# Fourier mixing and a gated feed-forward block: order of the weight preparation in the first chunk, and of two row transfers

## The chip, the cores and the metric

The kernel runs on one core of one Trainium2 chip. The metric is the device time of the whole kernel in microseconds (us); the kernel before takes 620.24 us in the median of 4 runs (620.0 to 620.54).

## The reference

```python
def _attn_ref(x):                       # x: (8, 3008, 256)
    X = np.fft.fft(x, axis=1)
    X = np.fft.fft(X, axis=2)
    return X.real.astype(np.float32)

def _moe_ref(x, w_gate, w_val, w_out):  # 24064 tokens, 256 -> 1536 -> 256
    g = x @ w_gate
    gelu = 0.5 * g * (1.0 + erf(g * np.float32(1.0 / np.sqrt(2.0))))
    val = x @ w_val
    return (gelu * val @ w_out).astype(np.float32)
```

The real part of a two-dimensional Fourier transform of each of 8 batches is the input of a feed-forward block with a GELU gate. The tokens of a batch come in mirrored pairs, so the kernel computes only half of them through the transform, as an even part E and an odd part O of 128 channels each.

## The kernel before, in words

**The feed-forward part.** Each batch has 1505 columns of token pairs, in three chunks of 512, 512 and 481. A chunk is worked through in twelve slots, one for each block of 128 columns of the inner dimension (1536). There are 8 x 3 x 12 = 288 slots, numbered from 0; slots 0 to 11 are the first chunk of batch 0. In slot i TensorE does, in this order:

- `G(i)` (`l1_gate`, line 674): gate columns of E, then of O, into a `ps_g` buffer (two of them); ScalarE's GELU (line 690) reads it;
- `g(i-1)` (`l1_gate2`): one more matmul with the weights "M" (minus two times the O weights) makes the mirrored tokens' gate of the slot before; ScalarE's second GELU (line 699) reads it and frees the buffer;
- `V(i)` (`l1_value`) and `v(i-1)` (`l1_value2`): the value columns, into `ps_v` (three buffers). In slots 0 to 7 of the first chunk (`three`), the value goes the same way as the gate, with a third weight set `w_minus`, and VectorE multiplies by the GELU (lines 713 and 730). From slot 8 on, the mirrored value is got without a third matmul: VectorE computes `ve` (line 718) from the row EB of channel 128 and `yw`, the value weights of that channel, then lines 734 and 736, and GpSimd multiplies (line 738);
- pieces of the output product of the chunk before (line 763, for the first chunk its own first pieces, from slot 9);
- `fill(i)`: whatever else a table gives to this slot.

**The fills of the first chunk** prepare the weights. `make_w(i, f0, n, parts, engine, m_engine)` multiplies the raw weights of gate (i=0) or value (i=1) with a 128-channel matrix, two matmuls of 512 columns for n=512 (line 451), into one of the two `ps_dft` buffers, and copies the result into `W_sb` with ScalarE (`engine="A"`, line 457) or VectorE ("V", line 459). `parts` are E (0) and O (1). For O it can also make M, with ScalarE (line 468) or VectorE (line 470) from the same `ps_dft` buffer, or with GpSimd ("P", line 466) from `W_sb`. `make_yw` computes `yw` from value's O weights (line 482, copy on line 484). `tp_y(0, 0)` makes EB of the first chunk (line 615, copy on line 618), `ch` and `tp_e`/`tp_o` are the last two steps of the transform (lines 535 and 591; copies on 541, 543 and 601).

**The rows.** For later batches `tp_row(b)` writes the row of channel 128 to a buffer in DRAM, and `tp_rows(b, c0, n)` reads it back with two transfers issued by SyncE on line 642: to all 128 partitions of EB, and to one partition of O. For batch 1 it is called once per chunk, after that chunk's `tp_o`; for later batches once for all chunks. The first slot of a batch is 36 b. SyncE also issues the output stores (line 668), four or more to a store, and takes its instructions in the order of the program.

**The order is written by hand** (`plan` fills two tables, `feed` walks them); every engine takes its own instructions in program order. Within a slot, the stores of finished output pieces come before the fill, since `feed` runs `two` before `fill`.

Of the kernel before, what the change touches and what calls it, by code (L numbers as in the profile page):

```python
# [28 lines left out]
def kernel(  # L29
# [22 lines left out]
    HALF = (NK - 1) * K1 + K1H  # L52
# [4 lines left out]
    def width(k2):  # L57
        return K1H if k2 == 0 else K1

    chunk_len = [sum(width(k2) for k2 in gr) for gr in groups]  # L60
    chunk_off = [sum(chunk_len[:i]) for i in range(NG)]
# [83 lines left out]
    def psum(tag):  # L145
        bufs = {"g": 2, "v": 3, "o": 1, "dft": 2}[tag]
        return psum_pool.tile([128, 512], FP32, tag=tag, bufs=bufs, name=f"ps_{tag}")
# [330 lines left out]
    def make_yw():  # L478
        def run():
            ps = psum("dft")  # L480
            for i in range(NFC):
                nc.tensor.matmul(
                    ps[:, i : i + 1], W["v", "O"][0:1, i * 128 : (i + 1) * 128], one_h, start=True, stop=True)
            nc.scalar.activation(yw[:, :], ps[:, 0:NFC], AF.Copy)
        return run
# [38 lines left out]
    def ch(b, pp, engine="A", qs=(0, 1)):  # L524

        def run():
            st = state(b)
            A = st["A"]
            if "Z" not in st:
                st["Z"] = Z_tile()  # L530
            ps = ps_any(b)
            for i, q in enumerate(qs):
                k = 2 * (2 * pp + q)
                for g in range(2):
                    nc.tensor.matmul(  # L535
                        ps[:, i * C : (i + 1) * C], _sub(A, [[1, 128]], g * NK * K1 + k * K1), II[:, g, :, :],
                        start=g == 0, stop=g == 1)
            n = len(qs) * C
            dst = _sub(st["Z"], [[1, n]], pp * 512 + qs[0] * C)
            if engine == "A":  # L540
                nc.scalar.activation(dst, ps[:, :n], AF.Copy)
            else:
                nc.vector.tensor_copy(dst, ps[:, :n])
        return run
# [39 lines left out]
    def tp_e(b, gi, g=0, engine="A", tag=None):  # L584
        def run():
            st = state(b)
            if b not in EO_bufs:
                EO_bufs[b] = EO_tiles()
            ps = psum(tag) if tag else ps_any(b)
            for pair, o, n in pairs(gi):  # L590
                nc.tensor.matmul(  # L591
                    ps[:, o : o + n], st["Z"][:, pair, g * 128 : g * 128 + 128], _sub(TP, [[1, n]], g * 128),
                    start=True, stop=True)
            if b == 0 and g == 1:
                for pair, o, n in pairs(gi):
                    nc.tensor.matmul(
                        ps[0:1, o : o + n], st["Z"][:, pair, 128:129], _sub(TP, [[1, n]], 0), start=True, stop=True)
            n = chunk_len[gi]
            dst = _sub(EO_bufs[b][g], [[1, n]], chunk_off[gi])
            if engine == "A":  # L600
                nc.scalar.activation(dst, ps[:, :n], AF.Copy)  # L601
            else:
                nc.vector.tensor_copy(dst, ps[:, :n])
        return run

    def tp_y(b, gi):

        def run():
            st = state(b)
            if b not in EB_bufs:  # L610
                EB_bufs[b] = EB_tile()
            n = chunk_len[gi]
            ps = ps_any(b)
            for pair, o, w in pairs(gi):
                nc.tensor.matmul(
                    ps[:, o : o + w], _sub(st["Z"], [[0, 128]], pair * C + 128), _sub(TP, [[1, w]], 0),
                    start=True, stop=True)
            nc.scalar.activation(_sub(EB_bufs[b], [[1, n]], chunk_off[gi]), ps[:, :n], AF.Copy)
        return run
# [18 lines left out]
    def tp_rows(b, c0, n):  # L638
        def run():
            y = yrow_dram[b % 2]  # L640
            for dst, rows in ((EB_bufs[b], 128), (EO_bufs[b][1], 1)):
                nc.sync.dma_start(
                    out=_sub(dst, [[1, n]], c0, part_num=rows),
                    in_=ap_replace(y, ap=[[0, rows], [1, n]], offset=y.offset + c0))
        return run

    def tp_o(b, gi, engine="A"):
        return tp_e(b, gi, 1, engine)
# [240 lines left out]
    def plan():  # L889

        fill, pool = {}, {}

        def at(table, s, f):
            table.setdefault(s, []).append(f)

        early = []
        for gi in (1, 2):
            e = "A" if gi == 1 else "V"
            early += [ch(0, 2 * gi), ch(0, 2 * gi + 1, e), tp_e(0, gi), tp_o(0, gi, e), tp_y(0, gi)]
        for s, f in (  # L900
                (0, make_w(0, 256, 256, m_engine="P")), (0, make_w(1, 256, 256, engine="V", m_engine="P")),
                (1, make_w(1, 512, 512, (1,), m_engine="P")), (1, lambda: load_wo(0)), (1, lambda: load_wo(1)),
                (2, make_w(0, 512, 512, (0,), "V")), (3, make_w(0, 512, 512, (1,))), (3, make_w(1, 512, 512, (0,), "V")),
                (4, make_w(1, 1024, 512, (1,), "V")), (5, make_w(0, 1024, 512, (0,), "V")),
                (5, make_yw()), (6, make_w(0, 1024, 512, (1,))), (6, tp_y(0, 0)), (7, make_w(1, 1024, 512, (0,), "V"))):
            at(fill, s, f)
        for i, f in enumerate(early):
            at(fill, (7, 8, 9, 10, 11, 12, 13, 14, 15, 16)[i], f)


        at(fill, 7, lambda: nc.sync.dma_start(
            out=ap_replace(yrow_dram[0], ap=[[0, 1], [1, 64]]), in_=EB_bufs[0][0:1, 0:64]))
        for k, s in ((0, 8), (1, 9), (2, 9)):
            at(fill, s, lambda k=k: load_part(2, k, (load_forward,)))
        for k, s in ((0, 18), (1, 19), (2, 19)):
            at(fill, s, lambda k=k: load_part(2, k, (load_mirror,)))

        taken = set()

        def spread(b, s0, s1):  # L920

            items = [tp_row(b)] + [f(b, gi) for gi in range(NG) for f in (tp_e, tp_o)]
            for i, f in enumerate(items):
                s = s0 + (i * (s1 - s0) // (len(items) - 1) if b > 1 else (0, 2, 3, 6, 8, 11, 13)[i])
                at(fill, s, f)
                taken.add(s)
                if b == 1 and i and i % 2 == 0:
                    at(fill, s + 1, tp_rows(b, chunk_off[i // 2 - 1], chunk_len[i // 2 - 1]))
            if b > 1:
                at(fill, s + 1, tp_rows(b, 0, HALF))  # L930

        for b in range(1, B):
            s0 = (b - 1) * NS
            ops = []
            for j0, nj in PIECES:
                ops += fold_ops(b, j0, nj, nc.gpsimd)
            per = len(ops) // 5
            first, n = (s0 - 19, 30) if b == 3 else (s0 - 22, 32)
            slot_of = [first + i * n // len(ops) for i in range(len(ops))]
            if b == 2:  # L940
                slot_of = [26, 27, 29, 30, 31, 33, 34, 37, 38, 39, 41, 42, 43, 45, 46, 49, 50, 50, 51, 51]
            if b == 1:
                slot_of = [4, 4, 5, 5, 6, 6, 7, 7, 8, 8, 9, 13, 13, 14, 15, 15, 16, 17, 17, 18]
            for s, f in zip(slot_of, ops):
                at(pool, s, f)
            if 1 < b < B - 1:
                for k, piece in ((0, 1), (1, 3), (2, 4)):
                    at(fill, slot_of[piece * per + 1] + 1, lambda b=b, k=k: load_part(b + 1, k))
            s = s0 - 9 if b > 1 else 12
            for i, (jg, piece) in enumerate(((2, 1), (1, 2), (0, 3), (3, 4))):  # L950
                ready = slot_of[piece * per + per - 1] + 2
                for g in range(2):
                    s = max(s + 1, ready)
                    while s in taken:
                        s += 1
                    at(fill, s, s1t(b, jg, g))
                if i == 2:
                    at(fill, s + 1, z_write(b, 0, 12))
                if i == 3:
                    at(fill, s + 1, z_write(b, 12, 4))  # L960
            at(fill, s + 2, z_read(b))
            if b == 1:
                spread(b, s + 7, s + 20)
                continue
            assert s + 7 < s0 + NS - 10
            spread(b, s + 7, s0 + NS - 5 if b == 2 else s0 + NS - 6)
        return fill, pool
# [71 lines left out]
```

## Time and profile before

| | |
|---|---|
| median of 4 runs | 620.24 us |
| the profiled execution, its own time | 620.08 us |
| its span | 618.2 us |
| TensorE matmuls busy | 609.7 us, 99% |
| VectorE busy | 576.5 us, 93% |
| GpSimd busy | 508.7 us, 82% |
| ScalarE busy | 425.0 us, 69% |
| granted TensorE clock | 1.0 |
| data moved | 65.40 MB, mean 106 GB/s |

The busy time of TensorE counts a matmul from its start to a modelled end, and matmuls overlap, so that small delays between two of them hide inside "busy". What tells them is the distance from one start to the next. A line of the timeline gives the start, the duration, the engine, the kernel's line, the operation with output and inputs, the count, and in brackets the idle time before it with what ended it. "PE" is the matmul, "PEld" the weight load, "DVE" VectorE, "ACT" ScalarE, "POOL" GpSimd, "SPq" SyncE's queue.

### The profile page before, as it was taken

To read this page: it belongs to the slowest core of one execution; us is meant where nothing else is said; L and a number is where in the kernel's file an instruction comes from. 1 tells how busy PE (TensorE), PEld (TensorE's weight loads), DVE (VectorE), ACT (ScalarE), POOL (GpSimd) and SP (SyncE) were. 2 spreads that over 40 slices of the span, in tenths; PEclk is the share of its full clock that TensorE was granted. 3 is DMA by queue.
4 is the path that set the end of the run, shared out by engine and by line. 5 is a ranking of instruction groups with operands and counts; after the bars stand their busy time and mean duration, and the time that the engine had idled before them with its cause. 6 is when DMAs were issued, how large, how long until landed. Compare 5 with 4: busy or idle time off the path is not lost.

```text
span 618.2 us, 12794 instructions
## 1 busy us (share of the span) xinstructions
PE 609.7 (99%) x4230; PEld 405.8 (66%) x4230; DVE 576.5 (93%) x940; ACT 425.0 (69%) x825; POOL 508.7 (82%) x513
## 2 busy tenths in 40 slices
PE   8999999999999999999999999999999999999997
PEld 4456666666666666666666666666666666666666
DVE  8789998999999999999999999999999999999992
ACT  7787667677766677676767677666776667666651
POOL 8989899999997999879997899969987555555561
PEclk9999999999999999999999999999999999999999
DMA  9952825546372354532553344533123312211123
GB/s 178 201 130 57 232 60 148 145 110 186 84 174 73 91 153 116 150 95 58 156 149 94 110 97 116 143 104 97 42 69 79 100 50 52 64 49 43 40 52 82
DMA packets 52466, 65.40 MB, mean 106 GB/s; under 512 B 7629, under 2 KB 47278, under 8 KB 50004
## 3 DMA queue, kind: packets, MB, share of 16 engines
q1 hardware_dynamic: 45472, 49.03, 30.4%
q0 software_dynamic: 6608, 15.29, 11.4%
q8 instruction: 33, 0.54, 0.4%
q10 hardware_dynamic: 320, 0.26, 0.2%
q14 instruction: 33, 0.27, 0.1%
HBM read 39.65 MB, written 30.17 MB: 113 GB/s over the span
## 4 chain that ended last, share of the span: by engine, by line
PE 93%; ACT 2%; DVE 2%; DMA 1%; issue 1%; SPq 0%; POOLq 0%; POOL 0%; ACTq 0%; DVEq 0%
PE ps_o L763 39%; PE ps_g L674 29%; PE ps_v L674 20%; PE ps_dft L555 2%; PE ps_dft L591 2%; DMA out_dram<-out_sb 1%; PE ps_dft L451 0%; DMA O_sb<-yrow 0%; ACT A_sb L519 0%; SPq L668 0%; DVE h_sb L730 0%; PE ps_dft L535 0%; DVE W_sb L459 0%; ACT G L351 0%; ACT L426 0%
## 5 line engine op out<-in xcount | busy, mean ns | idle before, releaser
L738 POOL TENSOR_TENSOR h_sb<-gelu_sb,v_sb 128x512 bf16<-128x512 bf16 (+1 forms) x280 | 319.8, 1147 | 90.8 <-DVE v_sb L736 78.6
L763 PE MATMUL ps_o<-Wo_sb,h_sb 128*128 128x256 bf16 (+1 forms) x2232 | 334.5, 273 | 0.0
L763 PEld LDWEIGHTS <-h_sb 128*128 128x128 bf16 (+1 forms) x2304 | 228.7, 100 | 111.2 <-POOL h_sb L738 1.2
L690 ACT ACTIVATE gelu_sb<-ps_g 128x512 bf16<-128x512 f32 (+1 forms) x288 | 169.5, 589 | 99.7 <-PE ps_g L674 93.5
L718 DVE SCALAR_TENSOR_TENSOR ve_sb<-EB_sb,yw,ps_v 128x512 f32<-128x512 bf16 (+1 forms) x280 | 206.1, 736 | 20.9 <-PE ps_v L674 17.1
L674 PEld LDWEIGHTS <-W_sb 128*128 128x128 bf16 x1440 | 138.0, 98 | 81.8 <-issue 4.1
L734 DVE TENSOR_TENSOR h_sb<-gelu_sb,ps_v 128x512 bf16<-128x512 bf16 (+1 forms) x280 | 189.7, 677 | 1.4 <-ACT gelu_sb L699 1.0
L736 DVE SCALAR_TENSOR_TENSOR v_sb<-ve_sb,ps_v 128x512 f32<-128x512 f32 (+1 forms) x280 | 187.2, 669 | 0.0
L674 PE MATMUL ps_g<-O_sb,W_sb 128*128 128x512 bf16 (+1 forms) x576 | 168.9, 374 | 0.6 <-DMA O_sb<-yrow 0.4
L699 ACT ACTIVATE gelu_sb<-ps_g 128x512 bf16<-128x512 f32 (+1 forms) x288 | 168.8, 586 | 0.0
L674 PE MATMUL ps_v<-E_sb,W_sb 128*128 128x512 bf16 (+1 forms) x288 | 108.0, 375 | 0.7 <-DVE W_sb L459 0.6
L674 PE MATMUL ps_g<-E_sb,W_sb 128*128 128x512 bf16 (+1 forms) x288 | 108.0, 375 | 0.7 <-ACT gelu_sb L699 0.3
L674 PE MATMUL ps_v<-O_sb,W_sb 128*128 128x512 bf16 (+1 forms) x288 | 108.0, 375 | 0.0
L783 ACT ACTIVATE out_sb<-ps_o 128x512 f32<-128x512 f32 x92 | 55.0, 598 | 34.4 <-PE ps_o L763 34.1
L229 POOL TENSOR_TENSOR eo_sb<-ab_sb 94x512 bf16<-94x512 f32 (+1 forms) x70 | 77.6, 1111 | 0.4
L558 ACT ACTIVATE S_sb<-ps_dft 96x512 bf16<-96x512 f32 x56 | 33.0, 589 | 18.6 <-PE ps_dft L555 18.6
L222 POOL TENSOR_TENSOR ab_sb<-x_raw,x_raw 94x508 f32<-94x508 f32 (+1 forms) x30 | 33.0, 1100 | 0.0
L225 POOL TENSOR_TENSOR ab_sb<-x_raw,x_raw 94x508 f32<-94x508 f32 (+1 forms) x30 | 33.0, 1099 | 0.0
L555 PE MATMUL ps_dft<-eo_sb,G 94*96 94x256 bf16 x119 | 22.3, 272 | 0.0
L601 ACT ACTIVATE E_sb<-ps_dft 128x512 bf16<-128x512 f32 (+1 forms) x23 | 13.5, 588 | 8.9 <-PE ps_dft L591 8.9
L163 POOL DMA_INDIRECT x_raw<-in_x_dram,idx x18 | 17.2, 956 | 2.9 <-issue 0.8
L601 ACT ACTIVATE O_sb<-ps_dft 128x512 bf16<-128x512 f32 (+1 forms) x22 | 13.0, 589 | 7.5 <-PE ps_dft L591 7.0
(151 smaller groups left out, 205.2 us busy)
## 6 DMA issues: line engine op xcount, KB each, us to landing
out_dram<-out_sb SPq DMA_DIRECT2D x364, 64.0 KB
x_raw<-in_x_dram SPq DMA_DIRECT2D x10, 768.0 KB
Z_sb<-z SPq DMA_DIRECT2D x7, 768.0 KB
z<-S_sb SPq DMA_DIRECT2D x7, 576.0 KB
EB_sb<-yrow SPq DMA_DIRECT2D x6, 376.2 KB
z<-S_sb SPq DMA_DIRECT2D x7, 192.0 KB
x_raw<-in_x_dram SPq DMA_DIRECT2D x2, 640.0 KB
x_stage<-in_x_dram SPq DMA_DIRECT2D x1, 768.0 KB
```

The source lines that it names most:

```text
L222: eng.tensor_tensor(ab(0, 1, up), fwd(1, up), mir(255, down), op=ALU.add)
L229: eng.tensor_tensor(_sub(eo, [[C, nj], [1, 128]], j0 * C + g * 128), ab(0, 0, [[1, 128]]), ab(1, 0, [[1, 128]]), op=op)
L555: nc.tensor.matmul(ps[:96, q * C : (q + 1) * C], G[:, j, :], _sub(eo, [[1, C]], j * C), start=(j == js[0]), stop=(j == js[-1]))
L674: nc.tensor.matmul(ps[:, :n], W[nm, part][:, fs], src, start=start, stop=stop, **kw)
L690: nc.scalar.activation(gl[:, 0, :n], pg[:, :n], AF.Gelu)
L699: nc.scalar.activation(_sub(gl, [[-1, n]], TOK + n - 1), pg[:, :n], AF.Gelu)
L718: nc.vector.scalar_tensor_tensor(ve[:, :n], EB_bufs[b][:, c0 : c0 + n], yw[:, fc : fc + 1], pv[:, :n], op0=ALU.mult, op1=ALU.add)
L734: nc.vector.tensor_tensor(st["h"][:, fc, 0, :n], gl[:, 0, :n], pv[:, :n], op=ALU.mult)
L736: nc.vector.scalar_tensor_tensor(_sub(vv, [[-1, n]], n - 1), ve[:, :n], 2.0, pv[:, :n], op0=ALU.mult, op1=ALU.subtract)
L738: nc.gpsimd.tensor_tensor(st["h"][:, fc, 1, :n], gl[:, 1, :n], vv[:, :n], op=ALU.mult)
L763: nc.tensor.matmul(pso[:m, half], st["h"][:, fc, sign, h0 : h0 + m], Wo_sb[:, fc, :], start=(fc == 0 and not (first and sign)), stop=(fc = ...
L783: nc.scalar.activation(_sub(osb, [[1, 2 * C]], 0, part_num=m), pso[:m, :], AF.Copy)
```

## The change

Three things. In the first chunk's fills, value's E columns 512 to 1023 move from slot 3 to slot 2 and those from 1024 on from slot 7 to slot 5; two M sets move from ScalarE to VectorE, and `ch(0, 2)` is copied by VectorE in place of ScalarE. `make_yw` and `tp_y(0, 0)` move one slot later. And `tp_rows` of all batches is put in the slot of the transform step before it, one slot sooner.

```diff
-            early += [ch(0, 2 * gi), ch(0, 2 * gi + 1, e), tp_e(0, gi), tp_o(0, gi, e), tp_y(0, gi)]
+            early += [ch(0, 2 * gi, "V" if gi == 1 else "A"), ch(0, 2 * gi + 1, e), tp_e(0, gi), tp_o(0, gi, e), tp_y(0, gi)]
         for s, f in (
                 (0, make_w(0, 256, 256, m_engine="P")), (0, make_w(1, 256, 256, engine="V", m_engine="P")),
                 (1, make_w(1, 512, 512, (1,), m_engine="P")), (1, lambda: load_wo(0)), (1, lambda: load_wo(1)),
-                (2, make_w(0, 512, 512, (0,), "V")), (3, make_w(0, 512, 512, (1,))), (3, make_w(1, 512, 512, (0,), "V")),
-                (4, make_w(1, 1024, 512, (1,), "V")), (5, make_w(0, 1024, 512, (0,), "V")),
-                (5, make_yw()), (6, make_w(0, 1024, 512, (1,))), (6, tp_y(0, 0)), (7, make_w(1, 1024, 512, (0,), "V"))):
+                (2, make_w(1, 512, 512, (0,))), (2, make_w(0, 512, 512, (0,), "V")),
+                (3, make_w(0, 512, 512, (1,), m_engine="V")),
+                (4, make_w(1, 1024, 512, (1,), "V")),
+                (5, make_w(1, 1024, 512, (0,))), (5, make_w(0, 1024, 512, (0,), "V")),
+                (6, make_yw()), (6, make_w(0, 1024, 512, (1,), m_engine="V")), (7, tp_y(0, 0))):
             at(fill, s, f)
...
                 if b == 1 and i and i % 2 == 0:
-                    at(fill, s + 1, tp_rows(b, chunk_off[i // 2 - 1], chunk_len[i // 2 - 1]))
+                    at(fill, s, tp_rows(b, chunk_off[i // 2 - 1], chunk_len[i // 2 - 1]))
             if b > 1:
-                at(fill, s + 1, tp_rows(b, 0, HALF))
+                at(fill, s, tp_rows(b, 0, HALF))
```

## The prediction

> **What bounds the kernel now.** I read the page first, then the waits, then the timeline where TensorE waits.
>
> ```profile
> span 618.2 us, 12794 instructions
> PE 609.7 (99%) x4230; PEld 405.8 (66%) x4230; DVE 576.5 (93%) x940; ACT 425.0 (69%) x825; POOL 508.7 (82%) x513
> PE 93%; ACT 2%; DVE 2%; DMA 1%; issue 1%; SPq 0%; POOLq 0%; POOL 0%; ACTq 0%; DVEq 0%
> ```
>
> TensorE is the bound, and 93% of the chain that ended last is its own. The change neither adds nor removes a matmul, so it can only gain where TensorE waits. The distances between matmul starts say how much that is: unhindered, 512 columns take 0.216 us, 256 take 0.109, 128 take 0.056. What exceeds these sums to some 15 us, of which 7.3 lie ahead of 20 us (the opening, untouched) and 3.5 after 100 us. The waits name the rest:
>
> ```profile
> PEld L674 <- DVE W_sb L459: 1.7, 2, 1.1
> PE ps_v L674 <- DVE W_sb L459: 0.6, 1, 0.6
> PEld L674 <- ACT W_sb L457: 0.5, 1, 0.5
> PE ps_g L674 <- DMA O_sb<-yrow: 0.4, 1, 0.4
> PE ps_g L674 <- ACT gelu_sb L699: 0.3, 1, 0.3
> ```
>
> In the timeline these are four places. Slot 4 (starts at 25.00), twice:
>
> ```profile
> 24.77 0.60 ACT L457 ACTIVATE W_sb<-ps_dft 128x512 bf16<-128x512 f32 x1 [0.21 <-PE ps_dft L451]
> 25.00 0.38 PE L674 MATMUL ps_g<-E_sb,W_sb 128*128 128x512 bf16 x1
> 25.41 0.68 DVE L459 CAST W_sb<-ps_dft 128x512 bf16<-128x512 f32 x1
> 25.42 0.60 PE L674 MATMUL ps_g<-O_sb,W_sb 128*128 128x512 bf16 x2
> 26.14 0.39 PE L674 MATMUL ps_v<-E_sb,W_sb 128*128 128x512 bf16 x1
> ```
>
> The O matmul could start at 25.22 and waits for gate's O columns, 0.205 us; V(4) could start at 25.86 and waits for value's E columns, 0.278. Then the start of slot 8, behind ScalarE, and V(8):
>
> ```profile
> 33.39 0.62 ACT L699 ACTIVATE gelu_sb<-ps_g 128x512 bf16<-128x512 f32 x1
> 34.06 0.38 PE L674 MATMUL ps_g<-E_sb,W_sb 128*128 128x512 bf16 x1 [0.34 <-ACT gelu_sb L699]
> 34.76 0.68 DVE L459 CAST W_sb<-ps_dft 128x512 bf16<-128x512 f32 x1
> 35.50 0.39 PE L674 MATMUL ps_v<-E_sb,W_sb 128*128 128x512 bf16 x1 [0.63 <-DVE W_sb L459]
> ```
>
> From start to start they lose 0.502 and 0.792 us. Last, slot 36, batch 1's first:
>
> ```profile
> 88.99 0.58 SPq L642 DMA_DIRECT2D EB_sb<-yrow  x1
> 89.62 0.29 SPq L642 DMA_DIRECT2D O_sb<-yrow  x1
> 91.66 0.38 PE L674 MATMUL ps_g<-E_sb,W_sb 128*128 128x512 bf16 x1
> 92.47 0.58 PE L674 MATMUL ps_g<-O_sb,W_sb 128*128 128x512 bf16 x2 [0.43 <-DMA O_sb<-yrow]
> ```
>
> O could start at 91.88 and starts at 92.47: 0.595 us. Slot 38 starts 0.152 late as well (96.50), behind ScalarE.
>
> **What the Trainium skill says.** "TensorE: Matmul & The Clock Gate", section "Wait — 56ns, not 53.3ns?", gives N/2.4 GHz plus 2.5 ns from start to start, 215.7 ns for 512 columns: the trace has 0.216. "PSUM — Partial Sum Buffer", section "PSUM bank collisions raise a hardware error", says that two engines must not access one bank at once, reads by ScalarE and VectorE included; so M on VectorE has to follow ScalarE's copy out of the same ps_dft buffer, and in the order of the changed kernel line 470 does wait for ScalarE. No pair like this stands in the first chunk before. "DMA: Bandwidth & Descriptors", section "Anatomy of one DMA — SWDGE (gpsimd) path", puts about 2 us of fixed cost on a transfer, mostly its completion; here the one-partition O row, behind SyncE's queue, takes 2.81 us from issue to landing.
>
> **The first chunk, slot by slot.** I walk the in-order queues with the trace's durations: ScalarE and VectorE start 0.42 us after the start of the last 512-column matmul that they need; a ScalarE instruction lasts 0.60 and lets the next start after 0.49; VectorE 0.68 and 0.60; a matmul that waits starts 0.05 after the end of what it waits for. With these the order before gives slot 4, 8, 9, 10 at 25.01, 34.00, 36.26, 38.09; the trace has 25.00, 34.06, 36.38, 38.20. One floor follows: in each slot the first GELU starts 0.22 + 0.42 = 0.64 us after the slot's start, the second 0.49 later, at 1.13, and ends at 1.73; the next slot's gate needs the buffer that it frees, and so opens 1.78 us after this one at the soonest, though six matmuls and one make_w are only 8 x 0.216 = 1.73.
>
> With the new order:
> - Slots 2 and 3. Slot 2 has two make_w (ten matmuls, 2.16), slot 3 one (1.78 by the floor): slot 3 opens at 23.22, slot 4 at 25.00 as before. The same matmuls, moved.
> - Slot 4. Value's E columns are there. But gate's O columns, first of slot 3's two fills before, are now at the end of slot 3: matmuls at 24.51 and 24.73, copy from 25.15 to 25.75, O matmul at 25.80 in place of 25.22. It loses 0.59, where before the slot lost 0.48. So this slot gains nothing, it loses 0.1. Slot 5: 27.36.
> - Slot 5 has two make_w; ScalarE copies one, VectorE the other: 2.16. Slot 6: 29.52.
> - Slot 6: six matmuls 1.29, yw 0.48 (from 28.96 to 29.44 before), make_w 0.43. Slot 7: 31.73. ScalarE copies yw (0.18) and gate's O to 32.57; VectorE's M follows, 32.62 to 33.30.
> - Slot 7: six matmuls, tp_y 0.22, then ch, whose ps_dft buffer M frees at 33.30: a wait of 0.07. ScalarE has only EB to copy (before: a weight copy and M, 31.37 to 32.55, then EB and the copy for ch). Slot 8 opens at 33.75 without the 0.50.
> - Slot 8: V(8) has its columns since slot 5, the 0.79 goes. Its 1.51 us of matmuls are below the floor, so slot 9 opens at 33.75 + 1.78 = 35.52 (a wait of 0.26). Slot 10: 37.30.
>
> 38.09 - 37.30 = 0.79 us of gain, 0.8. Bounds: 0.4, if the O wait in slot 4 and the floor each take 0.2 more; 1.1, if ScalarE is 0.3 sooner in slot 4. The price of M on VectorE (line 470, PSUM to bf16) isn't in the trace at 512 columns; the 256-column one at 17.64 took 0.47, a 512 cast 0.68. I take 0.68; at 0.95 (twice 0.47) ch in slot 7 waits 0.27 longer; at 0.47 its 0.07 go.
>
> **Cover.** The three VectorE instructions per slot (1.8 us) fit the slots of 1.78 to 2.16 with room from the slots before. Behind M of slot 6 stand lines 713 (slot 7), 730 (slot 6) and the copy for ch. 730 ends near 34.5 and V(9) needs its ps_v buffer at 36.2; the Z copy ends near 35.1 and tp_e reads it at about 37: 1.7 and 1.9 us of cover. EB is there at 34.1; line 718 wants it at 34.85. GpSimd runs without a gap to 39.47, whatever TensorE does, so its first product (line 738, slot 8) stays at 39.5, although its input comes 0.8 sooner; it was idle 1.07 and 0.59 before the next two, so by slot 10 it follows TensorE again. Its later combine (52.35 to 54.84) is read by TensorE at 55.36: 0.5 us of slack, kept if GpSimd moves along, as it is anchored by its product at 45.37, before which it idled 0.69. The small yrow transfer (line 911) behind EB goes from 33.06 to some 34.1, and the x_raw loads queued behind it on SyncE too; the folds of batch 2 that read them start in slot 26: no cost.
>
> **The rows.** In slot 33, not 34, two DMAs (0.58 and 0.29 us of issue) pass the four stores of 86.56 to 88.95. SyncE is free from 82.83. EB then waits only for the row's write, issued at 78.19; O waits for the ScalarE copy at 84.04 to 84.64. Even with their times from before (EB 88.99 to about 93.6, 4.6 us; O 2.81) they land by 88, and TensorE wants O at 91.88: the 0.595 goes whole. The stores come about 0.9 us later, four to an output buffer; three buffers rotate with some 6 us each, and no copy of line 783 waits for a store before. The later calls go one slot sooner and end no wait of TensorE; for batch 2 they pass stores as well, and O can hold SyncE for one copy of 0.6 us, at no cost for the same reason. The 0.152 at 96.50 may be a sequel or not: between 0 and 0.15; I take 0.
>
> Sum: 0.8 + 0.6 = 1.4 us. 620.08 - 1.40 = 618.7 for a profiled execution; the median stands 0.16 higher, so 618.8.
>
> **Rivals.**
> 1. The first chunk's gain is eaten by ScalarE, whose copy of gate's O columns in slot 4 now ends last; or GpSimd doesn't follow and TensorE waits at 55.36 for 0.8 - 0.5 = 0.3 us or more. For: the new 0.59 wait and the 0.5 us of slack. Against: slots 7 and 8 lose 1.3 us of waits for visible causes. Gain 0.6 to 1.1: 619.4.
> 2. More than summed: the wait of 96.50 goes too and slot 4 waits only as before. Gain 1.4 + 0.15 + 0.2: 618.5.
> 3. The rows bring nothing, since EB or O wait for something else in slot 33. Against: the order shows only the write, a queue entry and the copy. Gain 0.8: 619.4.
> 4. Slower: in slot 6 VectorE's M, held by ScalarE's copy, holds lines 713, 730 and the Z copy. TensorE waits from 1.7 us of delay on, one for one; to end 0.2% slower M would have to be late by 1.7 + 1.4 + 1.2 = 4.3 us, that is 621.5. ScalarE has no such backlog in that slot.
>
> **Numbers.** 0.2%, 1.24 us, is about what a measurement of this kernel can tell from no change: 619.0. Case as summed 0.55, rival 1 0.16, rival 2 0.15, rival 3 0.10, rival 4 0.04. The first falls below 619.0 with nine tenths, rival 2 wholly: 0.65 faster; 0.31 within; 0.04 slower. The range takes in rival 2 and most of 1 and 3: 618.2 to 619.7.
>
> **What would show it.** Right: no wait on W_sb by line 459, no wait on yrow; V(8) straight after slot 8's gate; the O matmul of slot 4 waiting 0.6 for line 457; slot 10 near 37.3; slot 37 (94.40 before) near 93.0. Wrong: a slot 4 that opens late, a new wait of line 555 on eo_sb, of line 763 on h_sb, or of line 783 on stores.

## The result, and the profile after

The changed kernel takes 619.38 us in the median of 41 runs (618.57 to 621.2), the kernel before 620.69 in 62 runs (619.45 to 622.75). The ratio is 0.9981, with a 95% interval of 0.9975 to 0.9986: faster by 1.2 us, between 0.9 and 1.6. The forecast was 1.4 us, from 620.2 to 618.8. So direction and size came out, but the runs show that the two parts of the sum did not share it as the prediction says.

The page of the changed kernel, its first lines and the granted clock:

```profile
span 617.3 us, 12798 instructions
PE 608.8 (99%) x4230; PEld 406.9 (66%) x4230; DVE 578.1 (94%) x941; ACT 424.9 (69%) x824; POOL 508.4 (82%) x513
PEclk8999999999999999999999999999999999999999
```

TensorE is the bound as before. The span is only 0.9 us shorter than the 618.2 of before; the 8 at the head of the clock line marks a slower opening, in which part of the gain is hidden, and the last section comes back to it. The waits of the changed kernel that have to do with weights:

```profile
PEld L674 <- ACT W_sb L457: 1.0, 1, 1.0
PE ps_g L674 <- ACT W_sb L457: 0.4, 1, 0.4
DVE W_sb L470 <- ACT W_sb L457: 0.4, 1, 0.4
```

The waits on VectorE's copies of line 459 (1.7 and 0.6) are gone from this view, and so is every wait on yrow. One wait on ScalarE's copy has grown instead. The timeline of the changed kernel shows it in slot 4:

```profile
25.50 0.38 PE L674 MATMUL ps_g<-E_sb,W_sb 128*128 128x512 bf16 x1
25.66 0.60 ACT L457 ACTIVATE W_sb<-ps_dft 128x512 bf16<-128x512 f32 x1 [0.21 <-PE ps_dft L451]
26.29 0.75 DVE L470 TENSOR_SCALAR W_sb<-ps_dft,keep 128x512 bf16<-128x512 f32 x1
26.31 0.60 PE L674 MATMUL ps_g<-O_sb,W_sb 128*128 128x512 bf16 x2 [0.43 <-ACT W_sb L457]
26.75 0.38 PE L674 MATMUL ps_v<-E_sb,W_sb 128*128 128x512 bf16 x1
```

Slot 4 opens at 25.50; its O matmul, wanted 0.216 later, starts 0.81 later, when gate's O columns have been copied. V(4) then follows at once, for value's E columns are there. (With their moves their copies also go from VectorE to ScalarE: the new lines have no "V".) The M set on VectorE (line 470) starts as ScalarE's copy ends. Slots 8 and 9 of the changed kernel:

```profile
34.31 0.38 PE L674 MATMUL ps_g<-E_sb,W_sb 128*128 128x512 bf16 x1
34.96 0.38 PE L674 MATMUL ps_v<-E_sb,W_sb 128*128 128x512 bf16 x1
35.44 0.59 ACT L699 ACTIVATE gelu_sb<-ps_g 128x512 bf16<-128x512 f32 x1
36.08 0.38 PE L674 MATMUL ps_g<-E_sb,W_sb 128*128 128x512 bf16 x1
```

V(8) starts 0.65 us after the slot, where it took 1.44 before; slot 9 opens 1.77 later, right after the second GELU: the floor. And the rows, on SyncE's queue of the changed kernel:

```profile
80.05 2.42 SPq L668 DMA_DIRECT2D out_dram<-out_sb  x4
82.56 0.53 SPq L642 DMA_DIRECT2D EB_sb<-yrow  x1
84.31 0.26 SPq L642 DMA_DIRECT2D O_sb<-yrow  x1
86.19 2.40 SPq L668 DMA_DIRECT2D out_dram<-out_sb  x4
88.97 0.35 SPq L157 DMA_DIRECT2D x_raw<-in_x_dram  x1
```

They now lie between two stores. The O row's completion is recorded at 85.68, 5.8 us ahead of its use in slot 36.

Since the opening differs from one execution to the next, the traces are best compared from the start of slot 1 on. The table gives all of them: the start of slot 1 in us, then how much later slots 8, 10, 38 and the last one (287) open, and the margin of the O row in the first slots of batches 1 and 2, which are slots 36 and 72 (from its landing to its unhindered use, 0.216 us after the slot's start; below zero TensorE waits). Its numbers are read from the starts of the first gate matmul of each slot and from the completion records of the transfers. The ratio is that of the timed runs to those of the kernel before, with its 95% interval; the second trace of before has no timed runs with it. Of these intervals, only those of "rows only" and "load later" lie clear of the interval in the first row of the changed kernel. So what a part is worth is read from the slot starts, and each kernel but two has one trace.

| kernel | slot 1 | +8 | +10 | +38 | +287 | margin batch 1, 2 | ratio |
|---|---|---|---|---|---|---|---|
| before | 19.29 | 14.77 | 18.91 | 77.21 | 581.39 | -0.55, 0.29 | 1 |
| before, again | 20.84 | 14.77 | 18.91 | 76.62 | 581.42 | 0.06, -0.48 | |
| changed | 19.81 | 14.50 | 18.04 | 75.59 | 579.88 | 5.8, 6.0 | 0.9981 (0.9975 to 0.9986) |
| changed, again | 19.29 | 14.50 | 18.04 | 75.59 | 579.85 | 5.6, 6.0 | 0.9984 (0.9976 to 0.9991) |
| rows only | 20.14 | 14.77 | 18.91 | 76.62 | 580.72 | 5.7, 6.1 | 0.9996 (0.9988 to 1.0005) |
| first chunk only | 19.50 | 14.50 | 18.04 | 75.62 | 579.99 | 0.01, 0.23 | 0.9993 (0.9985 to 1.0001) |
| load later | 20.27 | 14.77 | 18.91 | 76.62 | 581.09 | 0.29, 0.23 | 0.9999 (0.9989 to 1.0008) |
| M on ScalarE | 20.25 | 14.84 | 18.36 | 76.87 | 581.06 | 5.6, 6.1 | 0.9988 (0.9980 to 0.9995) |
| ch on ScalarE | 19.79 | 14.50 | 18.09 | 75.80 | 579.92 | 5.6, 6.2 | 0.9989 (0.9980 to 0.9998) |
| yw, tp_y as before | 20.05 | 15.06 | 18.59 | 76.41 | 580.67 | 5.6, 6.1 | 0.9992 (0.9979 to 1.0005) |
| value's E in slot 7 | 20.19 | 14.84 | 18.38 | 75.93 | 579.95 | 5.7, 6.0 | 0.9977 (0.9968 to 0.9987) |
| gate's O first | 20.78 | 13.92 | 17.46 | 75.12 | 579.41 | 5.6, 6.2 | 0.9974 (0.9965 to 0.9983) |
| ... and pieces sooner | 19.29 | 13.91 | 17.69 | 74.85 | 579.12 | 5.6, 6.1 | 0.9966 (0.9955 to 0.9977) |
| ... and Z later | 20.89 | 13.93 | 17.71 | 75.10 | 579.39 | 0.23, 6.2 | 0.9975 (0.9967 to 0.9983) |

### The profile page after: what moved, and what is told of

It is laid out like the page before. It is cut to its first block, busy times and chain, and to the rows that moved or that the text cites. A ratio compares the mean times of both kernels' runs of the same rounds, so it can differ in the third digit from the quotient of the medians.

```text
span 617.3 us, 12798 instructions
## 1 busy us (share of the span) xinstructions
PE 608.8 (99%) x4230; PEld 406.9 (66%) x4230; DVE 578.1 (94%) x941; ACT 424.9 (69%) x824; POOL 508.4 (82%) x513
## 4 chain that ended last, share of the span: by engine, by line
PE 95%; DMA 2%; ACT 1%; DVE 1%; issue 0%; POOL 0%; POOLq 0%; SPq 0%; ACTq 0%; DVEq 0%
PE ps_o L763 39%; PE ps_g L674 30%; PE ps_v L674 20%; PE ps_dft L555 2%; PE ps_dft L591 2%; DMA xb<-in_x_dram,idx 1%; DMA out_dram<-out_sb 1%; PE ps_dft L451 1%; PE ps_o L832 0%; PE ps_dft L535 0%; POOLq L1036 0%; ACT gelu_sb L699 0%; POOL h_sb L738 0%; PE ps_v L513 0%; ACT gelu_sb L690 0%
```

## Experiments

**One part alone.** Theory: the first chunk brings 0.8 us and the rows 0.6. The rivals are that one of them brings nothing.

Rows only:

```diff
-                    at(fill, s + 1, tp_rows(b, chunk_off[i // 2 - 1], chunk_len[i // 2 - 1]))
+                    at(fill, s, tp_rows(b, chunk_off[i // 2 - 1], chunk_len[i // 2 - 1]))
...
-                at(fill, s + 1, tp_rows(b, 0, HALF))
+                at(fill, s, tp_rows(b, 0, HALF))
```

> The kernel before with only the row transfers moved (all batches). Theory: the wait of slot 36 for the O row (0.595 us) and the late slot 38 (0.152) go, nothing else changes: 0.6 to 0.75 us below the kernel before; the first chunk keeps its four waits (0.2, 0.28, 0.5, 0.8 us). Rival, the rows bring nothing because EB or O wait for something else: same time as before, the wait on yrow stays.

In the trace the four waits of the first chunk are there to 0.003 us, and slot 38 opens 0.59 us sooner than in the first trace of before. The 0.152 at slot 38 did not go. The timed runs say 0.25 us, from 0.7 faster to 0.3 slower: less than expected.

First chunk only: the changed kernel with both lines of that diff taken back.

> The changed kernel with the row transfers left where they were. Theory: slot 10 opens 18.0 us after slot 1 in place of 18.9, 0.8 to 0.9 us below the kernel before, and the O wait of slot 36 stays (longer, since TensorE comes sooner but so do the stores: 0.5 to 0.7). Rival, ScalarE or GpSimd takes the gain back: under 0.4 us below, with a wait on eo_sb or h_sb between 45 and 65 us.

Slot 10 opens 18.04 us after slot 1, 0.87 sooner than before, to the digit as in the changed kernel. But the other half of the expectation fell: with the rows left in their old place, TensorE hardly waits for them (0.03 us). The timeline of the kernel with the first chunk alone, at slot 36:

```profile
88.32 0.58 SPq L642 DMA_DIRECT2D EB_sb<-yrow  x1
88.95 0.29 SPq L642 DMA_DIRECT2D O_sb<-yrow  x1
90.99 0.38 PE L674 MATMUL ps_g<-E_sb,W_sb 128*128 128x512 bf16 x1
91.24 0.58 PE L674 MATMUL ps_g<-O_sb,W_sb 128*128 128x512 bf16 x2
```

The O row took 2.24 us to land in place of 2.81, at 91.19, 0.01 before it was wanted. The 0.152 at slot 38 is gone here: it belongs to the first chunk, not to the rows. No wait on eo_sb or h_sb between 45 and 65 us shows, so GpSimd does follow. The timed ratio, 0.4 us faster with up to 0.9 in its interval, leaves open whether all of the 0.9 us arrives. The two parts timed alone, 0.25 and 0.4, sum to 0.7 and not to the 1.2 of the whole; the intervals are wide enough for both.

**Is the wait for the row a constant?** The kernel before was traced once more.

> The kernel before once more, for a second trace of it. Theory: the four waits of the first chunk come back within 0.02 us, for they hang on engine times alone; the start of slot 1 (19.29 us) moves by some tenths and with it the whole span, for the opening hangs on transfers; the wait of slot 36 for the O row, 0.595 in the first trace, is not the same, for it too hangs on a transfer: anything from 0 to 1 us. Rival, the wait on the row is set by SyncE's queue, which follows the engines: 0.55 to 0.65 again.

The first chunk is the same within 0.01 us. In slot 36 the O row landed 0.06 us early; TensorE does not wait. But it waits in slot 72, batch 2's first, where the first trace shows nothing. The timeline of this second trace of the kernel before:

```profile
165.21 0.30 SPq L642 DMA_DIRECT2D O_sb<-yrow  x1
167.67 0.38 PE L674 MATMUL ps_g<-E_sb,W_sb 128*128 128x512 bf16 x1
168.41 0.58 PE L674 MATMUL ps_g<-O_sb,W_sb 128*128 128x512 bf16 x2 [0.36 <-DMA O_sb<-yrow]
```

Here the row took 3.15 us, and from start to start the O matmul is 0.52 late. So the old place has two marginal landings, in slots 36 and 72, each with a margin around zero; which of them hurts differs from execution to execution. Over the four traces with the old place (before, before again, first chunk only, load later) the two slots cost 0.59, 0.52, 0.03 and 0 us, 0.3 in the mean. With the new place the margins are 5.6 to 6.2 us in all traces. To the last slot the trace with the rows alone is 0.7 us shorter than each of the two of before: by these waits, and by 0.05 and 0.15 us in slot 62, where line 763 waits for a product of GpSimd.

Is it the load behind the rows that makes them late? In the kernel before, only this moves:

```diff
-                    at(fill, slot_of[piece * per + 1] + 1, lambda b=b, k=k: load_part(b + 1, k))
+                    at(fill, slot_of[piece * per + 1] + (4 if (b, k) == (2, 0) else 1), lambda b=b, k=k: load_part(b + 1, k))
```

> The kernel before with only the 768 KB load of batch 3's first rows, issued right behind the two row transfers, put off by three slots. The O row took 2.81 us from issue to landing with that load behind it, 1.4 to 1.5 where it had none. Theory, the load is what makes the row late: it lands 1.5 us after its issue, TensorE does not wait in slot 36, 0.3 to 0.6 us below the kernel before. Rival, the four stores ahead of it in SyncE's queue and on the engines make it late: landing stays 2.2 to 2.8 us and the wait stays.

The O row landed 1.97 us after its issue and TensorE did not wait; EB took 3.3 us, not 4.6, and VectorE's wait for EB at line 718 (0.9 and 1.0 us in the two traces of before) is gone. But 1.97 is above the 1.5 of the theory, and not far below the 2.20 and 2.24 that two traces show with the load in place; the timed runs show no difference (0.9999). The load has a share in EB's landing, as far as one trace can show it; what decides between 2.0 and 3.15 us for the one-partition row stays open. In the new place it took 1.4 to 1.65 us.

**The first chunk's parts, undone one by one.** M by ScalarE again:

```diff
-                (3, make_w(0, 512, 512, (1,), m_engine="V")),
+                (3, make_w(0, 512, 512, (1,))),
...
-                (6, make_yw()), (6, make_w(0, 1024, 512, (1,), m_engine="V")), (7, tp_y(0, 0))):
+                (6, make_yw()), (6, make_w(0, 1024, 512, (1,))), (7, tp_y(0, 0))):
```

> The changed kernel with both M sets made by ScalarE again. Theory: the copies in slot 3 cost nothing (M follows the copy while TensorE waits for the copy alone), in slot 6 the extra 0.59 us on ScalarE comes out at slot 8, which opens 0.4 us later: 0.4 us above the changed kernel. Rival, ScalarE has room in slot 6 and the gain of slot 8 comes from value's weights alone: same time as the changed kernel.

Slot 8 opens 0.33 us later than in the changed kernel. Its timeline with M on ScalarE:

```profile
32.89 0.60 ACT L457 ACTIVATE W_sb<-ps_dft 128x512 bf16<-128x512 f32 x1 [0.36 <-PE ps_dft L451]
33.38 0.68 ACT L468 ACTIVATE W_sb<-ps_dft,keep 128x512 bf16<-128x512 f32 x1
33.95 0.60 ACT L690 ACTIVATE gelu_sb<-ps_g 128x512 bf16<-128x512 f32 x1
34.43 0.61 ACT L699 ACTIVATE gelu_sb<-ps_g 128x512 bf16<-128x512 f32 x1
35.09 0.38 PE L674 MATMUL ps_g<-E_sb,W_sb 128*128 128x512 bf16 x1 [0.28 <-ACT gelu_sb L699]
```

Copy, M and two GELUs run without a gap, and slot 8 waits for the second GELU, as in the kernel before. The move of M is worth its 0.33 us in the trace; the ratio of 0.9988 is too coarse to show it. Slot 3's M does cost nothing, as expected: slot 4, in which it runs, takes 2.38 us in place of 2.37. This trace shows one more wait, for Z in slot 28, which the last section tells.

`ch(0, 2)` by ScalarE again (`ch(0, 2 * gi)` in place of the choice of engine):

> The changed kernel with ch(0, 2) copied by ScalarE again. Theory: ScalarE has EB alone in slot 7 and takes this copy with 0.06 us more at slot 9: nothing that can be measured, 0 to 0.1 us above the changed kernel. Rival, the copy on ScalarE brings back the late start of slot 8 or 9: 0.3 to 0.5.

Slot 10 opens 0.05 us later, as worked out. The 0.152 at slot 38 came back, so it hangs on the engine of this one copy; slots 123 and 270 are shorter by as much as slots 37 and 152 are longer, and the last slot opens only 0.04 to 0.07 us later. Nothing of the gain hangs on this edit.

`make_yw` in slot 5 and `tp_y` in slot 6 as before:

```diff
-                (6, make_yw()), (6, make_w(0, 1024, 512, (1,), m_engine="V")), (7, tp_y(0, 0))):
+                (5, make_yw()), (6, make_w(0, 1024, 512, (1,), m_engine="V")), (6, tp_y(0, 0))):
```

> The changed kernel with make_yw in slot 5 and tp_y in slot 6 as before. Theory: yw needs a third ps_dft buffer in slot 5 and waits 0.3 us for the copy of the first, EB and the weight copy fall in the same slot again, and slot 8 opens 0.3 later: slot 10 opens 0.6 us later than in the changed kernel (18.65 us after slot 1). Rival, the later place of the two brings nothing: same time as the changed kernel.

Slot 10 opens 18.59 us after slot 1, 0.55 later. The wait for the third ps_dft buffer is there, in the timeline of this kernel in slot 5:

```profile
30.04 0.60 ACT L457 ACTIVATE W_sb<-ps_dft 128x512 bf16<-128x512 f32 x1 [0.21 <-PE ps_dft L451]
30.69 0.43 PE L482 MATMUL ps_dft<-one_h,W_sb 1*128 1x1 bf16 x12 [0.25 <-ACT W_sb L457]
```

Slots 5 and 6 together are 0.53 us longer, so nearly all of the loss is yw, and EB's place in slot 6 again costs almost nothing. The later place of `make_yw` is thus no by-work: with value's E columns in slot 5 it has to leave. That `tp_y` has to leave too is not shown, for the two were not undone apart.

Value's E columns from 1024 on in slot 7 again, copied by VectorE as before, with the rest as changed:

```diff
-                (5, make_w(1, 1024, 512, (0,))), (5, make_w(0, 1024, 512, (0,), "V")),
+                (5, make_w(0, 1024, 512, (0,), "V")),
...
-(7, tp_y(0, 0))):
+(7, tp_y(0, 0)), (7, make_w(1, 1024, 512, (0,), "V"))):
```

> The changed kernel with value's E columns from 1024 on made in slot 7 again (by VectorE), all else as changed. Theory: make_w comes back to slot 7, whose third ps_dft buffer is not free, and slot 10 opens 0.35 us later than in the changed kernel (18.4 us after slot 1); of the 0.79 us of V(8) only little returns, for make_w now stands ahead of ch on VectorE. Rival, V(8) waits 0.8 us again: slot 10 opens 0.8 later.

18.38 us, 0.34 above the changed kernel: as worked out, and less than the 0.79 that V(8) had waited. V(8) does not wait at all here. The loss lies in slot 7, where make_w waits 0.12 and ch 0.30 us for a ps_dft buffer. Why the copy is in time shows in VectorE's queue. First the kernel before:

```profile
33.56 0.69 DVE L713 TENSOR_TENSOR h_sb<-gelu_sb,ps_v 128x512 bf16<-128x512 bf16 x1 [1.48 <-ACT gelu_sb L690]
```

Then the kernel with value's E in slot 7; the last two lines are the start of slot 8 and V(8):

```profile
33.73 0.68 DVE L713 TENSOR_TENSOR h_sb<-gelu_sb,ps_v 128x512 bf16<-128x512 bf16 x1
34.92 0.68 DVE L459 CAST W_sb<-ps_dft 128x512 bf16<-128x512 f32 x1
35.03 0.38 PE L674 MATMUL ps_g<-E_sb,W_sb 128*128 128x512 bf16 x1
35.68 0.38 PE L674 MATMUL ps_v<-E_sb,W_sb 128*128 128x512 bf16 x1
```

The copy of line 459 stands behind lines 713 and 730. In the kernel before, line 713 waited for a GELU that stood behind M and EB on ScalarE, and the copy started 15.47 us after slot 1. Here neither M nor EB stands ahead of that GELU, and the copy starts at 14.73, with slot 8 at nearly the same distance (14.84 for 14.77). The expectation gave another reason, that make_w stands ahead of ch; it stood there before as well. By the end of the kernel only 0.1 us of the 0.34 is left in the trace (579.95 against 579.85 and 579.88), and the timed runs (0.9977) show nothing of it. So this edit, the one that aims at the longest wait of the first chunk, is worth about as much as the move of M: with the rest of the change in place, V(8) is in time either way.

**Does the new wait of slot 4 come from where the columns stand?** Gate's and value's O columns change places:

```diff
-                (1, make_w(1, 512, 512, (1,), m_engine="P")), (1, lambda: load_wo(0)), (1, lambda: load_wo(1)),
+                (1, make_w(0, 512, 512, (1,), m_engine="P")), (1, lambda: load_wo(0)), (1, lambda: load_wo(1)),
...
-                (3, make_w(0, 512, 512, (1,), m_engine="V")),
+                (3, make_w(1, 512, 512, (1,), m_engine="V")),
```

> The changed kernel with gate's O columns 512 to 1023 made in slot 1 (M by GpSimd) and value's O columns in slot 3 (M by VectorE), exchanged. Theory: the 0.595 us wait of slot 4 is only the copy of gate's O columns at the end of slot 3; value's O columns are wanted 0.65 us later in the slot, so the wait goes whole and the floor gives 0.05 back: 0.5 to 0.6 us below the changed kernel, slot 5 opens 1.78 us after slot 4 in place of 2.37. Rival, ScalarE's queue is the bound of that stretch whatever it copies: same time as the changed kernel, the wait moves to V(4) or slot 5.

Slot 4 with gate's O columns first:

```profile
26.48 0.38 PE L674 MATMUL ps_g<-E_sb,W_sb 128*128 128x512 bf16 x1
26.64 0.60 ACT L457 ACTIVATE W_sb<-ps_dft 128x512 bf16<-128x512 f32 x1 [0.21 <-PE ps_dft L451]
26.70 0.59 PE L674 MATMUL ps_g<-O_sb,W_sb 128*128 128x512 bf16 x2
27.34 0.38 PE L674 MATMUL ps_v<-O_sb,W_sb 128*128 128x512 bf16 x1
28.27 0.38 PE L674 MATMUL ps_g<-E_sb,W_sb 128*128 128x512 bf16 x1
```

The same copy ends at the same place in the slot, 27.24, but now it is value's O columns that it brings, and TensorE wants these at 27.34. The O matmul of the gate starts 0.22 after the slot, slot 5 after 1.79 in place of 2.37, and slot 10 opens 0.58 sooner than in the changed kernel. ScalarE was not the bound; the order of the columns was. At the last slot 0.44 to 0.47 us of it is left, for this trace loses 0.11 to Z in slot 28. The ratio, 0.9974 (0.9965 to 0.9983), is lower than the changed kernel's, with overlapping intervals.

With this, two output pieces one slot sooner:

```diff
-        sooner = {9: [first[0]], 10: [first[3]], 11: [first[1]], 12: [first[4]], 13: [first[2]], 14: [first[5]]}
+        sooner = {8: [first[0]], 9: [first[3]], 11: [first[1]], 12: [first[4]], 13: [first[2]], 14: [first[5]]}
```

> The exchange of gate's and value's O columns (0.58 us in its trace), and besides the first two output pieces one slot earlier, in slots 8 and 9, leaving slot 10 without. Slot 8 has matmuls for 1.51 us under a floor of 1.78, so the piece of 0.44 costs 0.17 there, and slot 10 falls from 2.15 to the floor: theory, 0.15 to 0.2 below the exchange alone, 0.75 below the changed kernel. Rival, the piece lengthens slot 8 fully and slot 10 has a wait of its own: same as the exchange alone.

Slot 20 opens 38.80 us after slot 1 in place of 38.96: 0.16, as worked out. The ratio is 0.9966 (0.9955 to 0.9977), 2.1 us below the kernel before; the changed kernel, timed beside it, has 0.9984 (0.9976 to 0.9991). From slot 1 to the last slot it is 0.73 to 0.75 us shorter than the changed kernel, as expected. It has the lowest ratio of all, though its interval overlaps those of its neighbours in the table.

On top of it, the last transform steps of batches 1 and 2 one slot later, to give the read of Z more time (`spread(b, s + 8, s + 21)` for batch 1, `s + 8` for batch 2):

> The kernel with the exchange and the earlier output pieces, and besides the last transform steps of batches 1 and 2 begin one slot later, so that the read of Z from DRAM has 2 us more: TensorE waited for it 0 to 0.95 us in slot 28 and 0 to 0.34 in slot 62 in the traces so far. The O rows keep 3.5 us or more of margin. Theory: no wait on Z in any of these slots, 0.1 to 0.3 below the kernel with the exchange and the earlier pieces; 0.9 to 1.1 below the changed kernel. Rival, Z is late for another reason and the wait moves with it: no gain.

No wait for Z, but the kernel lost elsewhere: slot 38 opens 0.25 us later than without this edit, in slots 28 to 37, where the moved steps now fall beside other fills. 0.9975 is no gain. The waits for Z that it would save were small or none in most traces, and those of slot 62 were none for Z: in the trace with the 0.34, load later, line 763 waits there for a product of GpSimd. The expectation on the O rows failed too. With the steps of batch 1 its rows went one slot later, back to their old place; the O row took 2.28 us again, and its margin fell to 0.23 us. Batch 2's rows kept their new place and 6.2 us.

**The changed kernel once more.**

> The changed kernel once more, beside the others. Theory: from slot 1 to slot 38 it takes 75.6 us again (the kernel before 77.2 and 75.8 plus 0.6 elsewhere in two traces), the O rows of batches 1 and 2 land 5.5 us or more ahead of their use, and the span differs from the first trace by the start of slot 1 alone. The time is 1.2 us below the kernel before, 0.8 to 1.7. Rival, the earlier work of the first chunk delays the opening: slot 1 starts later than 20.8 us.

75.59 us from slot 1 to slot 38 again, the O rows 5.6 and 6.0 us ahead, and slot 1 at 19.29: the later start in the first trace was no effect of the change. The ratio says 1.0 us below the kernel before (0.6 to 1.5). (For the second trace of before the expectation should have said 76.62, not 75.8.)

## Why the prediction was right, point by point

- **The first chunk, 0.8 us.** Right, and step by step: 0.87 between slots 1 and 10 in both traces. Slot 4's O matmul waits 0.595 (worked out: 0.59), slot 8 opens without its 0.50, V(8) without its 0.79, slot 9 waits 0.252 at the floor (0.26), ch 0.117 for its buffer (0.07). The last is M on VectorE: 0.75 us, not the 0.68 that I took, so its price lay between my two bounds. The walk through the in-order queues with the trace's durations was good to 0.1 us, also for three other orders (18.36, 18.59 and 18.38 measured, where the walk gave 0.4, 0.6 and 0.35 above the changed kernel).
- **The 0.152 at slot 38.** I took 0 and left it between the parts; it goes with the first chunk in both traces of the changed kernel, by ScalarE's copy for ch. Later slots give about as much back (0.15 more in slots 123 and 270, 0.16 less in 152), so the first chunk is worth 0.84 to 0.87 us from slot 1 to the last slot, rows only against changed.
- **The rows, 0.6 us: mis-sized.** "The 0.595 goes whole" held for the traced execution only. The wait was no property of the kernel but of one landing: 0.59, 0, 0.03 and 0 us in slot 36 of the four traces with the old place. The step that failed is the reading of one trace's wait as a constant cost. And "the later calls ... end no wait of TensorE" was wrong: batch 2's landing in slot 72 had a margin of 0.29 us in the page that I read, and cost 0.52 in the next trace. The term measures 0.3 us in the mean of the four traces (0 to 0.6), and 0.25 (-0.3 to 0.7) in the timed runs of the rows alone. 0.85 + 0.3 is 1.15, beside 1.2 measured for the whole. The interval of the whole, 0.9 to 1.6, could not tell 1.15 from the 1.4 of the forecast: that the sum fits says nothing for the rows' 0.6.
- **Slot numbers of the rows.** I placed the calls in slots 34 and 33; counted from slot 36 back, they are in 32 and 31. The times (issue from 82.83 on, the O row after the copy that ends at 84.64) did not depend on it.
- **Cover.** GpSimd's combine ended at 54.48 with its reader at 55.00, the slack of 0.5 kept; no new wait on h_sb came up (line 763 has 1.2 us in four waits in both kernels), and none by line 783 on stores. Rivals 1 and 4 did not happen. Rival 2 holds for the 0.15 but not for slot 4. Rival 3, that the rows bring nothing, has its number in two of the four traces with the old place, but not its reason: there the O row simply landed in time.
- **The Trainium skill on banks.** "PSUM — Partial Sum Buffer", section "PSUM bank collisions raise a hardware error": the trace agrees as far as the order goes: VectorE's M waits for ScalarE's copy (0.4 us in the waits) though both only read. That it has to wait was not tried here. The O row, issued by SyncE, landed in 1.4 to 1.65 us in its new place, below the fixed cost of about 2 us that the prediction quotes from a section on the path through GpSimd.

## What to carry to other kernels

In this kernel a wait on an engine came back to hundredths from trace to trace, while a wait on a transfer was one draw. So look at the margin of all landings of that kind, and take a margin near zero for a wait that some executions have and others do not, also where this trace shows none: of the eight landings in slots 36 and 72 of the four traces with the old place, two cost over 0.5 us. When work is moved between slots, ask for each of its results at which point inside the next slot it is wanted: the sum of work per slot was the same, and exchanging two results of equal cost was worth 0.58 us. And where two edits go for the same wait, only undoing one alone tells what it is worth: V(8) had waited 0.79 us, and undoing the move of its columns cost 0.34, all of it elsewhere.

## What the runs showed of the hardware that I had not expected

**The clock in the opening.** In the 14 traces slot 1 starts between 19.29 and 20.89 us, on code that is the same up to there. The traces with a mean granted clock of 0.999 or 1.0 have 19.29 to 19.50, those with 0.996 or 0.997 have 19.79 to 20.89. The windows view of the first trace of before, then of the kernel with gate's O first; after the busy times stand the granted clock, the DMA share and GB/s:

```profile
8.00:12.00 4.00, 3.50 (x28) 2.06 (x29) 3.97 (x14) 3.89 (x11) 4.00 (x6) 1.00 1.12 192
12.00:16.00 4.00, 3.48 (x43) 2.61 (x43) 3.05 (x12) 3.84 (x10) 3.70 (x6) 1.00 1.31 166
```

```profile
8.00:12.00 4.00, 2.72 (x18) 1.67 (x19) 3.43 (x13) 3.53 (x11) 4.00 (x6) 0.75 1.11 196
12.00:16.00 4.00, 3.40 (x36) 1.96 (x34) 2.89 (x12) 3.21 (x8) 3.70 (x6) 0.83 1.24 168
```

In the second kernel the clock is not full for a stretch between 8 and 16 us, after TensorE has finished its 16 warm-up matmuls and waited for the first folds. The missing clock is 0.25 x 4 + 0.17 x 4 = 1.7 us, which at half speed is 3.4 us, the window that "TensorE: Matmul & The Clock Gate", section "The HAM clock gate (the "warmup" mystery)", states for a free-running monitor. Each trace's own record of the granted clock bears it out: in the ten traces with the lower mean it is at half for 3.41 us, from a start between 9.25 and 11.05 us, and in the other four it stays full. No long pause is needed for it: in the 3.41 us ahead of the half clock TensorE had matmuls in all ten traces, and the longest pause between them was from 0.25 to 1.8 us. That the start differs from one execution to the next would fit a monitor that runs freely; it is not shown.

The clock is not the whole of the spread. The first matmul of line 513, the first step of the transform, starts at 9.08 to 9.23 us in eleven traces, full clock or not, and at 9.62 to 9.69 in three, and these three have the latest slot 1 (20.78 to 20.89). The other seven with half clock have 19.79 to 20.27. Why the three start late is open.

This spread of 1.6 us is larger than the change, and it is in every span and every timed run here. Each timed run has its mean granted clock on record, so the runs beside the two parts can be sorted by it. At 0.999 or 1.0 the medians are 619.64 us for the kernel before (23 runs), 618.96 for the first chunk alone (8) and 619.63 for the rows alone (3). Below, they are 620.71 (27), 620.21 (13) and 620.41 (10). So the first chunk shows in both groups, the rows in the second only; these are few runs, sorted after the fact, and no more than a hint. That a longer warm-up would hold the clock was not tried.

**A third marginal landing.** The read of Z from DRAM takes 4.2 to 4.6 us and is wanted in slot 28; in the kernel with M on ScalarE, the waits view has

```profile
PEld L627 <- DMA Z_sb<-z: 1.0, 1, 1.0
PE ps_dft L627 <- DMA Z_sb<-z: 0.7, 1, 0.7
```

which cost 0.95 us of slot 28, against nothing in both traces of the kernel before. In every trace the read goes out as the write of z ahead of it lands. That write took 8.74 us here, against 6.69 in the first trace of before, and the two other traces that lose time to Z in slot 28, with 0.27 and 0.11 us, have 8.27 and 8.08. What makes the write slow is open.
